# The second product of one batch in matmuls of 256 columns instead of 512, two to a bank

## The chip, the cores and the metric

One core of one Trainium2 chip. The metric is the time of one execution on the device, in microseconds (us); given is the median of a few executions. The engines are TensorE (PE in the profile; its weight loads have a row of their own, PEld), VectorE (DVE), ScalarE (ACT), GpSimd (POOL) and SyncE (SP, which issues nearly all DMAs here).

## The reference

Eight batches of 576 tokens with 8 heads of 64 go through an attention in two steps over 32 packed queries, and then through a feed-forward layer with the gate h * sigmoid(1.702 h). Everything is float32.

```python
def sm_attn(qq, kk, vv):
    s = scale * np.matmul(qq, kk.transpose(0, 1, 3, 2))
    s = s - np.max(s, axis=-1, keepdims=True)
    a = np.exp(s)
    a = a / (np.sum(a, axis=-1, keepdims=True) + 1e-09)
    return np.matmul(a, vv)
p_packed = sm_attn(p, k, v)
out = sm_attn(q, p_packed, p_packed)
...
h = x @ w_in                              # x: 4608 x 512, w_in: 512 x 2048
g = h * (1.0 / (1.0 + np.exp(-1.702 * h)))
return (g @ w_out).astype(np.float32)     # w_out: 2048 x 512
```

## The kernel before

The kernel works batch by batch (B = 8), but its steps are written out by hand in one long table, `order`, in which steps of neighbouring batches alternate: while the feed-forward part of batch 4 runs, the attention of batch 5 and 6 is prepared between its products. Each entry of the table is a function with its arguments, such as `(out_mm, 4, 0, 2)`, and each engine carries out its instructions in the order in which the table issues them.

Precision comes from splitting: a float32 operand is held as a rounded upper part and a lower part, both in the format F32R, and a product is the sum of three: upper x upper, upper x lower, lower x upper.

The attention's last step and the first product of the feed-forward layer are joined: per batch and 512 columns of `w_in` a small matrix m is made (`m_chunk`, PE line L437, tile `psm`), and `h_mm` (L605) multiplies it by the attention's weights. There are 16 column blocks f of 128 and two halves of 288 tokens. Each `h_mm` is six matmuls of 288 columns, with weights of 128x128, into one PSUM bank (tile h, two buffers).

ScalarE then takes the tanh of h (`h_tanh`, L613), VectorE forms the gate (`h_gate`, L595), and two more steps write the upper and lower part of g (`h_upper`, lines L117 and L119; `h_lower`, L592), tiles `ghi` and `glo`, each 128 rows of f by 512 tokens, three buffers. The 64 tokens of a batch beyond 512 are set aside (`h_over`) and worked on in pairs of batches (`over_mm`, tile `acc_over`).

The second product is `out_mm(b, f, i)`: for batch b, block f and token block i (0 to 3, 128 tokens each) it calls `product` (L660 to L667), which issues three matmuls: weights `ghi`, `ghi` and `glo` (128x128 columns of that token block), moving operand the upper, lower and upper part of `w_out`'s block f, all 512 output columns at once. All 16 f of a token block add up in one PSUM bank, `acc0` to `acc3`; the first matmul at f = 0 has start set, the last at f = 15 has stop set. `out_take` then copies the bank to SBUF and `store` writes it out. So a batch has 16 x 4 x 3 = 192 such matmuls. `columns(part)` gives 0:256 for 0, 256:512 for 1 and 0:512 for None; it was there for loading weights by halves.

Of the kernel before, what the change touches and what calls it, by code (L numbers as in the profile page):

```python
# [21 lines left out]
def kernel(  # L22
# [31 lines left out]
    nc = tc.nc  # L54

    P = 128
# [8 lines left out]
    NF = DF // P  # L65
    FC = 512
# [5 lines left out]
    KLAST = S - (KC - 1) * P  # L72
    DEC = 3
    MB = 2
    LATE = [(B - 1, 2)]
    SCALE = 1.0 / float(D) ** 0.5

# [90 lines left out]
    wo = {}  # L168
# [5 lines left out]
    def columns(part):  # L174
        return slice(0, FC) if part is None else slice(part * FC // 2, (part + 1) * FC // 2)
# [276 lines left out]
    def m_upper(b, fc, eo, part=None, engine=nc.scalar):  # L452
        if not part and (b, fc) in LATE:
            if ("late", b, fc) not in st:
                st["late", b, fc] = wk.tile(
                    [P, 2, 2, FC], F32R, tag="late", name=f"late_{b}_{fc}"
                )
            st["m", b, fc, eo] = [st["late", b, fc][:, eo, i, :] for i in range(2)]
        elif not part:
            st["m", b, fc, eo] = [  # L460
                wk.tile([P, FC], F32R, tag=f"{tag}{eo}", name=f"{tag}_{b}_{fc}_{eo}", bufs=MB)
                for tag in ("mhi", "mlo")
            ]
        at = columns(part)
        move(engine, st["m", b, fc, eo][0][:, at], st["bank", "m", b, fc, eo, part][:, at])
# [111 lines left out]
    gs = {}  # L577
    accs = {}
# [81 lines left out]
        src = over_g[pair, i].rearrange("p f t -> p (f t)")  # L660
        lower(g_tiles(("over", pair, i)), 0, src, engine)

    def product(acc, g, f, at, start, stop):
        for i, (part, gp) in enumerate(((0, g[0]), (1, g[0]), (0, g[1]))):
            nc.tensor.matmul(  # L665
                acc, gp[:, at : at + P], wo[f][:, part, :],
                start=(start and i == 0), stop=(stop and i == 2),  # L667
            )

    def acc_bank(i, name):  # L670
        return ps_acc.tile([P, FC], F32, tag=f"acc{i}", name=f"acc{i}_{name}")
# [3 lines left out]
    def out_mm(b, f, i):  # L675
        if f == 0:
            accs[i] = acc_bank(i, f"{b}")
        product(accs[i], gs[b, f], f, i * P, f == 0, f == NF - 1)

    def out_take(b, i, engine=nc.scalar):  # L680
        taken[b, i] = o = o_tile(f"o_{b}_{i}")
# [5 lines left out]
    def over_mm(pair, i):  # L687
        g = gs["over", pair, i]
        if i == 0:
            accs[0] = acc_bank(0, f"over_{pair}")  # L690
        for n in range(CF):
            f = CF * i + n
            product(accs[0], g, f, n * P, f == 0, f == NF - 1)
# [5 lines left out]
    def over_store(pair, k, engine=nc.sync):  # L699
# [38 lines left out]
        (h_upper, 0, 0, 0), (h_lower, 0, 0, 0), (m_chunk, 0, 0, (bank_b, bank_b), 1),  # L738
        (m_upper, 0, 0, 0, 1, dve), (load_w, 5), (bias1, 1, 0), (begin_w, 5), (join_w, 5),
        (h_mm, 0, 0, 1), (m_lower, 0, 0, 0, 1), (out_mm, 0, 0, 0), (h_mm, 0, 1, 1),  # L740
        (h_upper, 0, 1, 0), (h_lower, 0, 1, 0), (load_w, 8), (h_tanh, 0, 0, 1), (out_mm, 0, 0, 1),
        (h_over, 0, 0), (h_gate, 0, 0, 1), (m_upper, 0, 0, 1, 1), (m_lower, 0, 0, 1, 1),
        (h_mm, 0, 2, 0), (upper_w, 5), (h_tanh, 0, 1, 1), (h_gate, 0, 1, 1), (h_over, 0, 1),
        (h_upper, 0, 0, 1), (h_lower, 0, 0, 1, dve), (out_mm, 0, 0, 2), (out_mm, 0, 0, 3),
        (load_w, 6), (begin_w, 6), (join_w, 6), (h_tanh, 0, 2, 0), (lower_w, 5),
        (h_upper, 0, 1, 1), (load_w, 7), (begin_w, 7), (h_gate, 0, 2, 0), (join_w, 7),
# [698 lines left out]
```

## Time and profile before

| | |
|---|---|
| median of 3 runs | 698.31 us (698.3 to 698.85) |
| span of the profiled execution, first to last instruction | 695.4 us (no other time of that execution is given) |
| mean granted TensorE clock | 0.999 |
| matmuls, weight loads | 5022, 5022 |
| of them in the second product | 1536 (8 x 192), and 192 in `acc_over` |
| second product of batch 4 in the trace | about 366 to 444 us |

How to read the rows that follow: a group's row gives line, engine, operation, tiles (out<-in), shapes and count, then busy time, the mean duration of one in ns, and the engine's idle time before them. The chain of waits follows the work that ended last back to the start; here its pieces are listed in order of time as start, length, what, and a count. Matmuls are pipelined: one starts long before the record of the one before it has ended, so a record's duration is not what a matmul costs in a row. F32 matmuls (not F32R) have two records each.

### The profile page before, as it was taken

Reading aid. Unit: us, or ns where it says so; the run is one execution under the profiler, and the core shown is the slowest. Engines: PE = TensorE matmul, PEld = TensorE weight load, DVE = VectorE, ACT = ScalarE, POOL = GpSimd, SP = SyncE. Lnnn points to the kernel's source line nnn. Section 1 sums busy time; section 2 is a strip of 40 time slices with the busy share of each in tenths; the row PEclk is TensorE's granted clock in tenths of the full one; section 3 lists DMA queues with packets and bytes.
Section 4 is the critical chain, followed back from the end, with each engine's and each line's share of the span. In section 5 each row is a group of like instructions: output and inputs, shape, how many; then the busy total and the mean of one; then the engine's idle time right before and its main releaser. Section 6 shows DMA issues by size and latency. Waiting matters only on the chain.

```text
span 695.4 us, 12968 instructions
## 1 busy us (share of the span) xinstructions
PE 685.3 (99%) x5022; PEld 561.1 (81%) x5022; DVE 439.1 (63%) x1111; ACT 258.1 (37%) x620; POOL 96.1 (14%) x115
## 2 busy tenths in 40 slices
PE   7999999999999999999999999999999999999997
PEld 5688788888888888887888878888888887878885
DVE  4988784536555467555686477766785647855443
ACT  3876554423314324433323233332232333333220
POOL 2554372112300224011000000000000000000000
PEclk9999999999999999999999999999999999999999
DMA  8989703432101511064000623034200160010001
GB/s 336 375 307 240 283 1 107 93 113 77 65 1 30 184 65 54 16 155 160 1 31 6 156 56 131 16 110 111 96 16 1 37 177 1 23 40 1 1 15 61
DMA packets 55260, 65.18 MB, mean 94 GB/s; under 512 B 35808, under 2 KB 40864, under 8 KB 54176
## 3 DMA queue, kind: packets, MB, share of 16 engines
q1 hardware_dynamic: 55120, 64.23, 29.2%
q8 instruction: 40, 0.66, 0.4%
q14 instruction: 20, 0.16, 0.1%
q10 hardware_dynamic: 80, 0.13, 0.0%
HBM read 50.78 MB, written 13.57 MB: 93 GB/s over the span
## 4 chain that ended last, share of the span: by engine, by line
PE 93%; DMA 3%; DVE 1%; issue 1%; SPq 1%; ACT 0%; DVEq 0%; ACTq 0%
PE acc L665 50%; PE h L605 28%; PE acc_over L665 5%; PE psm_None L437 4%; DMA aT<-aside 2%; PE pspv L408 1%; PE ps L250 1%; PE ps L495 1%; DMA k<-pk 1%; PE warm L125 1%; SPq L384 1%; DMA aside<-xb 0%; DVE ghi L119 0%; DVE x L506 0%; PE pst L345 0%
## 5 line engine op out<-in xcount | busy, mean ns | idle before, releaser
L665 PE MATMUL acc<-wo,ghi 128*128 128x512 f32 x1024 | 322.9, 397 | 0.0
L665 PEld LDWEIGHTS acc<-wo,ghi 128*128 128x128 f32 x1024 | 179.8, 188 | 40.2 <-issue 11.2
L613 ACT ACTIVATE g<-h 128x288 f32<-128x288 f32 x256 | 104.1, 410 | 278.1 <-PE h L605 262.1
L665 PE MATMUL acc<-wo,glo 128*128 128x512 f32 x512 | 202.0, 395 | 0.0
L595 DVE SCALAR_TENSOR_TENSOR g<-g,h 128x288 f32<-128x288 f32 (+1 forms) x256 | 104.9, 415 | 116.4 <-ACT g L613 115.8
L605 PE MATMUL h<-ahi,mhi 128*128 128x288 f32 x496 | 140.1, 298 | 0.3 <-DVE g L595 0.3
L605 PE MATMUL h<-ahi,mlo 128*128 128x288 f32 x496 | 138.9, 296 | 0.0
L665 PEld LDWEIGHTS acc<-wo,glo 128*128 128x128 f32 x512 | 96.2, 188 | 22.8 <-POOL glo L592 0.4
L605 PEld LDWEIGHTS h<-ahi,mhi 128*128 128x128 f32 x496 | 93.4, 188 | 16.2 <-DVE x L506 4.9
L605 PE MATMUL h<-alo,mhi 128*128 128x288 f32 x496 | 105.2, 293 | 0.0
L605 PEld LDWEIGHTS h<-ahi,mlo 128*128 128x128 f32 x496 | 93.5, 189 | 6.9
L592 DVE TENSOR_TENSOR glo<-g,ghi 128x224 fp32r<-128x224 f32 (+1 forms) x183 | 76.1, 427 | 14.8 <-ACT ghi L117 10.8
L592 POOL TENSOR_TENSOR glo<-g,ghi 128x224 fp32r<-128x224 f32 (+1 forms) x73 | 55.5, 767 | 191.3 <-DVE ghi L119 88.1
L605 PEld LDWEIGHTS h<-alo,mhi 128*128 128x128 f32 x496 | 79.7, 188 | 0.1
L117 ACT CAST ghi<-g 128x288 fp32r<-128x288 f32 (+1 forms) x142 | 55.2, 403 | 54.4 <-DVE g L595 47.6
L595 DVE SCALAR_TENSOR_TENSOR over<-g,h 128x64 f32<-128x64 f32 x128 | 27.0, 214 | 30.6 <-ACT g L613 30.1
L471 DVE TENSOR_TENSOR mlo<-psm_None,mhi 128x512 fp32r<-128x512 f32 x60 | 40.6, 684 | 5.2 <-ACT mhi L117 4.9
L119 DVE CAST ghi<-g 128x224 fp32r<-128x224 f32 (+1 forms) x114 | 35.9, 320 | 7.0 <-PE acc L665 1.4
L665 PE MATMUL acc_over<-wo,ghi_over 128*128 128x512 f32 x128 | 39.9, 393 | 0.0
L117 ACT CAST mhi<-psm_None 128x512 fp32r<-128x512 f32 x45 | 26.2, 584 | 29.3 <-PE psm_None L437 29.3
L437 PE MATMUL psm_None<-w_in,PT 64*32 64x512 f32 x496 | 33.4, 597 | 0.0
L665 PEld LDWEIGHTS acc_over<-wo,ghi_over 128*128 128x128 f32 x128 | 23.6, 188 | 4.8
(95 smaller groups left out, 475.9 us busy)
## 6 DMA issues: line engine op xcount, KB each, us to landing
q<-q SPq DMA_DIRECT2D x16, 576.0 KB, 5.8
v<-v SPq DMA_DIRECT2D x8, 1024.0 KB, 6.2
o<-o SPq DMA_DIRECT2D x32, 256.0 KB, 2.6
raw<-w_out SPq DMA_DIRECT2D x16, 511.8 KB, 6.5
raw<-w_in SPq DMA_DIRECT2D x12, 511.8 KB, 8.9
k<-pk SPq DMA_DIRECT2D x8, 640.0 KB, 4.3
k<-pk SPq DMA_DIRECT2D x8, 576.0 KB, 6.9
aside<-xb SPq DMA_DIRECT2D x56, 72.0 KB, 2.3
```

Of the source, the lines that this page charges most:

```text
L117: nc.scalar.copy(dst, src)
L119: engine.tensor_copy(dst, src)
L125: nc.tensor.matmul(t[:, :P], ident, ident, start=True, stop=True)
L250: nc.tensor.matmul(bank[32 * j : 32 * j + 32, :NH], kq["p", b][rows(eo), j, :], kq["k", b][rows(eo), half, j, :], start=True, stop=True,)
L384: nc.sync.dma_start(d[:, :, NP * eo + j, :], src.rearrange("t (g n) -> t g n", n=NPK))
L437: nc.tensor.matmul(banks[eo][32 * j : 32 * j + 32, columns(part)], PT[rows(eo), j, :], w_in_sb[fc][rows(eo), j, columns(part)], start=True ...
L471: nc.vector.tensor_tensor(lo, bank[:, at], hi.bitcast(F32), op=ALU.subtract)
L592: engine.tensor_tensor(lo, src, hi.bitcast(F32), op=ALU.subtract)
L595: nc.vector.scalar_tensor_tensor(dst, th, 1.0, h, op0=ALU.add, op1=ALU.mult)
L605: nc.tensor.matmul(h[:, :NH], m[eo][part][:, fo : fo + P], a[:, eo * NH : (eo + 1) * NH], start=(n == 0), stop=(n == len(terms) - 1),)
L613: nc.scalar.activation(g, st["h", b, f, half][:, :NH], AF.Tanh, scale=1.702)
L665: nc.tensor.matmul(acc, gp[:, at : at + P], wo[f][:, part, :], start=(start and i == 0), stop=(stop and i == 2),)
```

## The change

For batch 4 alone (`NARROW = 4`) each matmul of the second product becomes two of 256 columns that write the left and the right half of the same bank. The loop over the halves is inside the loop over the three terms, so the order of a product is upper-upper left, upper-upper right, upper-lower left, and so on. The two halves have the same weights, and each has its own weight load. The start flag is on the first half of the first term alone, the stop flag on the last half of the last.

```diff
+    NARROW = 4
...
-    def product(acc, g, f, at, start, stop):
+    def product(acc, g, f, at, start, stop, pieces=(slice(0, FC),)):
         for i, (part, gp) in enumerate(((0, g[0]), (1, g[0]), (0, g[1]))):
-            nc.tensor.matmul(
-                acc, gp[:, at : at + P], wo[f][:, part, :],
-                start=(start and i == 0), stop=(stop and i == 2),
-            )
+            for k, cs in enumerate(pieces):
+                nc.tensor.matmul(
+                    acc[:, cs], gp[:, at : at + P], wo[f][:, part, cs],
+                    start=(start and i == 0 and k == 0), stop=(stop and i == 2 and k == len(pieces) - 1),
+                )
...
-        product(accs[i], gs[b, f], f, i * P, f == 0, f == NF - 1)
+        pieces = (columns(0), columns(1)) if b == NARROW else (slice(0, FC),)
+        product(accs[i], gs[b, f], f, i * P, f == 0, f == NF - 1, pieces)
```

What this does to the order on PE, at two places. First, PE at the first product of batch 4 (f = 0, i = 2), which stands between two `h_mm`; `acc2_4` is bank 2 of batch 4, and in brackets stands what a matmul waits for. Before:

```order
L605 MATMUL h_4_0_2_4347<-alo_4_0_4286,mhi_4_0_1_4148 128x288
L665 MATMUL acc2_4_4358<-wo0_388,ghi_4_0_4319 128x512 [waits Activation_49]
L665 MATMUL acc2_4_4358<-wo0_388,ghi_4_0_4319 128x512
L665 MATMUL acc2_4_4358<-wo0_388,glo_4_0_4320 128x512 [waits DVE_49]
L605 MATMUL h_4_1_2_4365<-ahi_4_1_4186,mhi_4_0_0_3986 128x288 [waits DVE_49]
```

and with the change:

```order
L606 MATMUL h_4_0_2_4347<-alo_4_0_4286,mhi_4_0_1_4148 128x288
L667 MATMUL acc2_4_4358<-wo0_388,ghi_4_0_4319 128x256 [waits Activation_49]
L667 MATMUL acc2_4_4358<-wo0_388,ghi_4_0_4319 128x256 x3
L667 MATMUL acc2_4_4358<-wo0_388,glo_4_0_4320 128x256 [waits DVE_49]
L667 MATMUL acc2_4_4358<-wo0_388,glo_4_0_4320 128x256
L606 MATMUL h_4_1_2_4368<-ahi_4_1_4186,mhi_4_0_0_3986 128x288 [waits DVE_49]
```

Three matmuls became six at the same place, and the waits stay with the first that needs the tile. The second place is PE at the first products of batch 5 in banks 0, 1 and 3, whose columns are not halved. Before:

```order
L665 MATMUL acc0_5_5269<-wo0_388,ghi_5_0_5220 128x512 x2
L665 MATMUL acc0_5_5269<-wo0_388,glo_5_0_5221 128x512
L665 MATMUL acc0_5_5269<-wo1_498,ghi_5_1_5246 128x512 [waits DVE_49]
L665 MATMUL acc0_5_5269<-wo1_498,ghi_5_1_5246 128x512
L665 MATMUL acc0_5_5269<-wo1_498,glo_5_1_5247 128x512 [waits DVE_49]
L665 MATMUL acc1_5_5286<-wo0_388,ghi_5_0_5220 128x512 x2
L665 MATMUL acc1_5_5286<-wo0_388,glo_5_0_5221 128x512
L665 MATMUL acc3_5_5294<-wo0_388,ghi_5_0_5220 128x512 [waits Activation_49]
```

and with the change:

```order
L667 MATMUL acc0_5_5461<-wo0_388,ghi_5_0_5403 128x512 [waits PE_49]
L667 MATMUL acc0_5_5461<-wo0_388,ghi_5_0_5403 128x512
L667 MATMUL acc0_5_5461<-wo0_388,glo_5_0_5404 128x512
L667 MATMUL acc0_5_5461<-wo1_498,ghi_5_1_5438 128x512 [waits DVE_49]
L667 MATMUL acc0_5_5461<-wo1_498,ghi_5_1_5438 128x512
L667 MATMUL acc0_5_5461<-wo1_498,glo_5_1_5439 128x512 [waits DVE_49]
L667 MATMUL acc1_5_5478<-wo0_388,ghi_5_0_5403 128x512 [waits PE_49]
L667 MATMUL acc1_5_5478<-wo0_388,ghi_5_0_5403 128x512
L667 MATMUL acc1_5_5478<-wo0_388,glo_5_0_5404 128x512
L667 MATMUL acc3_5_5486<-wo0_388,ghi_5_0_5403 128x512 [waits PE_49,Activation_49]
```

The work and its order are the same (only the numbers of the tiles differ); three matmuls now also wait for a piece of PE's own earlier work. The orders of DVE, ACT, POOL and SP do not change.

## The prediction

> **What bounds the kernel now.** I read the page first: the busy shares and the granted clock.
>
> ```profile
> span 695.4 us, 12968 instructions
> PE 685.3 (99%) x5022; PEld 561.1 (81%) x5022; DVE 439.1 (63%) x1111; ACT 258.1 (37%) x620; POOL 96.1 (14%) x115
> PEclk9999999999999999999999999999999999999999
> ...
> PE 93%; DMA 3%; DVE 1%; issue 1%; SPq 1%; ACT 0%; DVEq 0%; ACTq 0%
> ```
>
> TensorE (PE) is busy for 99% of the span at a clock that is never throttled, it holds 93% of the chain that ended last (the last row), and every matmul has a weight load of its own (5022 of each). A busy matmul row is not yet a matmul row at its peak, so the next view was the table of stretches, for the stretch that holds the second product of batch 4 (366 to 444 us), together with the groups of that stretch, which show that it holds exactly the 192 matmuls that the change touches.
>
> ```profile
> 366.00:444.00 78.00, 78.00 (x594) 63.80 (x593) 50.27 (x132) 27.39 (x69) 0.00 (x0) 1.00 0.28 78
> L665 PE MATMUL acc<-wo,ghi 128*128 128x512 f32 x128 | 40.3, 396 | 0.0
> L665 PE MATMUL acc<-wo,glo 128*128 128x512 f32 x64 | 25.3, 395 | 0.0
> ACT g L613 <- PE h L605: 38.1, 23, 4.9
> ```
>
> The columns of the first row are stretch, its length, then busy time and count of PE, PEld, DVE, ACT and POOL. PE is busy for all 78.00 us; it waits for nobody there. The last row, from the waits of that stretch, shows the other direction: ScalarE stands idle for 38.1 us until PE delivers h. So nothing in this stretch hides PE time: each nanosecond that PE needs more or less moves the end by as much.
>
> The 395 ns of a matmul in the groups is a latency, start to modelled end; matmuls overlap. What the path pays is the distance from one to the next, and that is read from the chain of waits in order of time (start, us, what). The long unbroken runs of batch 4's stretch:
>
> ```profile
> 371.82 2.79 PE acc L665 x12
> 377.90 4.79 PE acc L665 x21
> 388.83 2.80 PE acc L665 x12
> 392.43 2.08 PE acc L665 x9
> 396.12 3.41 PE acc L665 x15
> 417.76 4.82 PE acc L665 x21
> 430.80 4.89 PE acc L665 x21
> 442.04 2.09 PE acc L665 x9
> ...
> 385.65 1.61 PE h L605 x12
> 394.51 1.61 PE h L605 x12
> 410.14 1.60 PE h L605 x12
> 416.20 1.56 PE h L605 x12
> 422.58 1.56 PE h L605 x12
> 429.21 1.59 PE h L605 x12
> 438.17 1.58 PE h L605 x12
> 440.45 1.58 PE h L605 x12
> ```
>
> The eight runs of 512-column matmuls (acc) hold 120 in 27.67 us: 230.6 ns each. The eight runs of 288-column matmuls (h, the first product, same engine, same kinds of operands, also 128 rows by 128 columns of weights) hold 96 in 12.69 us: 132.2 ns each.
>
> **The change part by part.** It removes 192 matmuls of 512 columns (16 f x 4 token blocks x 3 terms) with their 192 weight loads, and adds 384 of 256 columns with 384 loads. Each pair of halves has the same weights, and they are loaded for each half again.
>
> *The matmuls.* No 128-row matmul of 256 columns in this number format stands in the trace, so its price is drawn through the two widths that do. From 288 to 512 columns the distance grows by 230.6 - 132.2 = 98.4 ns over 224 columns, 0.439 ns a column; going 32 columns below 288 takes off 14.1 ns and gives 118.1 ns. Two of those are 236.2 ns, against 230.6 for the one that they replace: 5.6 ns more. The same line says what that is: at no columns it still stands at 5.7 ns, a fixed price of a matmul that is now paid once more. 192 x 5.6 ns = 1.07 us. All of it is on the path, since PE is never idle in the stretch.
>
> The uncertainty of this term comes from the spread between runs. The steepest line takes the slowest acc run (4.89 us for 21: 232.9 ns) and the fastest h run (1.56 us for 12: 130.0): 0.459 ns a column, 115.3 ns for 256, a pair at 230.6 and so 2.3 ns less than one: -0.44 us. The flattest takes the fastest acc run (3.41 us for 15: 227.3) and the slowest h run (1.61 for 12: 134.2): 0.416 a column, 120.9 for 256, 14.5 ns more a pair: +2.8 us. I take the pooled value, because mixing the fastest of one kind with the slowest of the other is a worst case, and keep both ends for the range.
>
> The Trainium skill, page "TensorE: Matmul & The Clock Gate", section "Back-to-back issue gap", puts the warm distance at N/2.4 + 2.5 ns, hence a fixed price of 2.5 ns. By that rule the sum would be 192 x 2.5 = 0.48 us (an estimate from that page). It gives 215.8 ns for 512 columns where the rows here show 230.6, so I go by the rows.
>
> *The weight loads.* A load lasts 188 ns in its record, longer than the new distance, so I looked for the nearest that loads can follow each other. Before the steady part, warm-up matmuls of 128 columns run back to back:
>
> ```profile
> 16.16 1.41 PEld L125 LDWEIGHTS warm<-ident 128*128 128x128 f32 x12 [0.47 <-issue]
> L665 PEld LDWEIGHTS acc<-wo,ghi 128*128 128x128 f32 x1024 | 179.8, 188 | 40.2 <-issue 11.2
> ```
>
> Twelve loads of 128x128 f32 cover 1.41 us; less the 0.19 us of the last one's record, eleven distances make 1.22 us, 111 ns each. Loads are therefore pipelined, and one every 118 ns can be had, with 7 ns in hand. The matmul hides the next load as now: 0 us. If that cover were gone (loads of the operands here slower than these), the price is the first rival's.
>
> *Instructions and waits.* In the order of the instructions only PE differs. The waits that the 512-column matmuls carried sit on the first half of each term, so no half waits longer than its whole did. Three first matmuls of batch 5 newly name an earlier piece of PE's own work, and one matmul of batch 5 no longer does; that work lies before them in the same queue. Price between 0 and 3 x 0.11 us (a load that cannot be pulled ahead, from the 111 ns above) = 0.33 us; I take 0, since waits of this kind stand before some 45 matmuls already, and PE is busy for 99% of the span with them. Program code is fetched by DMA: 384 instructions at the 63 bytes that the page's rows give,
>
> ```profile
> q8 instruction: 40, 0.66, 0.4%
> q14 instruction: 20, 0.16, 0.1%
> ```
>
> 0.82 MB for 12968, are 24 KB more beside queues that are busy for 0.5%: 0 us. ACT, DVE and the stores of batch 4 get their data up to 1 us later; ACT has 38.1 us of waiting in hand there, and the next work of PE doesn't ask for a store.
>
> *The sum.* 695.4 us of span + 1.07 = 696.5 us. The median of the runs shown, 698.31, lies 2.9 us over that span; nothing of that part is touched. 698.31 + 1.07 = 699.4 us. That is 0.15%, and 0.2% (1.4 us) is about what a measurement of this kernel can tell from no change: the forecast is "within".
>
> **The rivals.** *The weight loads become the bound, and it is slower.* The mechanism: the 132.2 ns of an h matmul might be not its columns but a load that can't be had sooner; then a 256-column matmul also costs 132.2 ns, a pair 264.4, 33.8 ns more than one, 192 x 33.8 = 6.5 us: 704.8 us. It decides as soon as loads of these tiles can't follow within 118 ns, and costs half as much (701.6 us) if they need 124. For it speaks that the record of a load, 188 ns, is longer than the distance; against it the 111 ns of the warm-up loads, of the same 128x128 four-byte shape. Chance 0.10. The Trainium skill, page "Perfetto Trace Analysis", section "Identifying the Most-Contended Engine", has TensorE's headroom judged by the busy share of the weight loads; by that rule a stretch that goes from 63.80 of 78 us towards all of it would have no headroom left, which bears on this rival.
>
> *It is faster.* The excess of a long matmul might not be a straight line: if the fixed price is hidden by shorter matmuls and a half runs at the 111 ns of the closest rows, a pair takes 222, 8.6 ns less than one: -1.65 us, 696.7 us. For it speaks that runs of the same width differ by 2.5% already (227.3 to 232.9), so something beside the columns is in the distance; against it that h, with shorter matmuls, has more time per column, not less (132.2/288 = 0.459 against 230.6/512 = 0.450). Chance 0.05.
>
> *The instruction sequencer becomes the bound.* The stretch issues 594 + 593 = 1187 matmuls and loads in 78.0 us, 65.7 ns each, and would issue 1571. If that were what one takes, down to the 65.0 ns of the fastest h run (24 in 1.56 us), they need 102 to 103 us, 24 to 25 us more: 722 to 723 us. Against it, a run of 80 matmuls with their loads in 1.25 us,
>
> ```profile
> 400.31 1.25 PE pspv L408 x80
> ```
>
> 160 instructions at 8 ns each, though a queue may have held part of them ready. Chance 0.03. The Trainium skill has a sentence that speaks for it, on the page "TensorE: Matmul & The Clock Gate", section "Wait — 56ns, not 53.3ns?": with hardware decode off the sequencer spends about 62 ns on each matmul; were a load to cost the same, that is 97 us for the stretch (an estimate from that page). No row here says which mode this is.
>
> *Half-width matmuls lose the full rate.* The f32 warm-up matmuls take 111 ns for 128 columns, 0.87 ns a column against h's 0.46. If 256 columns of this format fell to that rate, a half would take 222 ns, a pair 444, 192 x 213 ns = 41 us: 739 us. Nothing below 288 columns shows it either way. Chance 0.02.
>
> **How the numbers follow.** The forecast, the fixed price paid twice, has 0.80. Its own bounds are 698.31 - 0.44 = 697.9 and 698.31 + 2.8 = 701.1. I let the range reach to 701.6, half the first rival's price, and leave out the rest of it (about 0.05), the faster case (0.05), the two far ones (0.05) and a tail of 0.05: 697.9 to 701.6. Slower by over 0.2% means above 699.7, an extra of 7.3 ns a pair and so 119.0 ns a half: only 0.9 ns above my value. I give that 0.30 of the forecast's 0.80 (0.24), and nearly all of the three slower rivals (0.15): 0.39. Faster by over 0.2% needs less than 696.9: most of the faster rival, 0.04. Within: 0.57.
>
> **What would show it.** In the profile after, the stretch of batch 4 still has PE busy throughout, about 1.1 us longer; the chain's acc runs there hold 18 or 24 where 9 or 12 stood and give 116 to 121 ns a matmul; h stays at 132. Loads at 118 ns apart with matmuls starting on them say the first rival is gone. Distances of 130 or more in the halves, with the load as what PE waits for, say that I was wrong by it; 111 or less says the faster case; equal distances of load and matmul that hold in the h runs of that stretch too would be the sequencer. If batch 5's first products show PE idle, the three new waits were not free.

## The result, and the profile after

| | before | after |
|---|---|---|
| median of 17 runs | 698.31 us (696.82 to 699.39) | 699.78 us (698.9 to 703.05) |
| ratio, 95% interval | | 1.0025 (1.0016 to 1.0034) |
| span of the profiled execution | 695.4 us | 697.2 us |

The change costs 1.47 us by the medians, and between 1.1 and 2.4 us by the interval. The forecast was 1.07 us more, 0.15%; the measured 0.25% lies on the slower side of the 0.2% that were to be told from no change, but its interval, 0.16% to 0.34%, reaches to both sides of them.

The page after, span and busy times:

```profile
span 697.2 us, 13353 instructions
...
PE 686.7 (98%) x5214; PEld 571.1 (82%) x5214; DVE 439.2 (63%) x1111; ACT 258.4 (37%) x620; POOL 95.7 (14%) x115
```

There are 192 matmuls and 192 loads more, as the order said, and the other engines do what they did. The table of stretches, for the stretch of batch 4 (stretch, length, busy time and count of PE, PEld, DVE, ACT, POOL, then the granted clock, DMA share and GB/s):

```profile
366.00:446.00 80.00, 80.00 (x788) 75.06 (x787) 50.37 (x132) 27.41 (x69) 0.00 (x0) 1.00 0.27 76
```

PE is still never idle there. What grew is its own work, and the weight loads went from 63.80 of 78 us to 75.06 of 80. The chain of waits in order of time shows where (start, us, what); first and last piece of batch 4's second product and the runs that answer to those shown of before:

```profile
367.16 0.71 PE acc L667 x6
...
372.38 2.85 PE acc L667 x24
...
378.54 5.03 PE acc L667 x42
...
389.74 2.88 PE acc L667 x24
...
393.41 2.15 PE acc L667 x18
...
397.15 3.60 PE acc L667 x30
...
419.25 5.04 PE acc L667 x42
...
429.61 1.41 PE acc L667 x12
431.02 1.60 PE h L606 x12
432.63 4.98 PE acc L667 x42
...
440.10 1.58 PE h L606 x12
...
443.99 2.13 PE acc L667 x18
```

The eight runs that correspond hold 240 halves in 28.66 us: 119.4 ns each, where the prediction had 118.1. A pair takes 238.8 ns, 8.2 more than the 230.6 of one matmul before. The h runs stay at 132 ns (1.58 for 12). From the start of the first piece to the end of the last, 367.16 to 446.12, are 78.96 us. Before, the stretch ran from the start of the row below to the end of the run at 442.04 (shown in the prediction), 366.67 to 444.13:

```profile
366.67 0.69 PE acc L665 x3
```

77.46 us, so the stretch grew by 1.50 us, about as much as the medians differ by. Added up over the chain of the stretch, all acc pieces take 46.46 us where they took 45.01, 1.45 more for the 192 pairs; the 186 h matmuls take 25.07 and 25.06, and the other pieces are the same to 0.01 us. The two spans differ by 1.8 us, because batch 4 also begins 0.5 us later, before any changed instruction has run, and what follows the stretch is about 0.1 us shorter. The groups of the loads in that stretch show one more thing, the mean ns of a record, after and before:

```profile
L667 PEld LDWEIGHTS acc<-wo,ghi 128*128 128x128 f32 x252 | 34.7, 190 | 1.4 <-DVE x L120 0.8 <-issue 0.5
L667 PEld LDWEIGHTS acc<-wo,glo 128*128 128x128 f32 x125 | 19.4, 191 | 0.0
```

```profile
L665 PEld LDWEIGHTS acc<-wo,ghi 128*128 128x128 f32 x128 | 22.5, 188 | 4.8 <-DVE x L119 0.8 <-issue 0.5 <-ACT ghi L117 0.2
```

A load lasts 2 to 3 ns longer where the matmul beside it has 256 columns. It is small, but it asks a question that the prediction passed over: is the price one of the matmul, as the word "fixed price of a matmul" had it, or one of the load that each matmul brings with it? In a straight line through two widths the two look the same.

### The profile page after: what moved, and what is told of

Read it like the earlier page. It is cut to its first block, busy times and chain, and to the rows that moved or that the text cites. A ratio compares the mean times of both kernels' runs of the same rounds, so it can differ in the third digit from the quotient of the medians.

```text
span 697.2 us, 13353 instructions
## 1 busy us (share of the span) xinstructions
PE 686.7 (98%) x5214; PEld 571.1 (82%) x5214; DVE 439.2 (63%) x1111; ACT 258.4 (37%) x620; POOL 95.7 (14%) x115
## 4 chain that ended last, share of the span: by engine, by line
PE 95%; DMA 2%; issue 1%; DVE 1%; ACT 0%; SPq 0%; DVEq 0%
PE acc L667 51%; PE h L606 29%; PE acc_over L667 5%; PE psm_None L438 4%; PE ps L251 1%; DMA raw<-w_in 1%; PE pspv L409 1%; PE ps L496 1%; DMA k<-pk 1%; PE warm L126 0%; PE psm L438 0%; DVE mlo L472 0%; SPq L158 0%; ACT mhi L118 0%; DVE g L596 0%
## 5 line engine op out<-in xcount | busy, mean ns | idle before, releaser
L667 PE MATMUL acc<-wo,ghi 128*128 128x512 f32 (+1 forms) x1152 | 323.7, 371 | 0.0
L667 PEld LDWEIGHTS acc<-wo,ghi 128*128 128x128 f32 x1152 | 192.4, 188 | 36.9 <-issue 11.2
L667 PE MATMUL acc<-wo,glo 128*128 128x512 f32 (+1 forms) x576 | 202.4, 369 | 0.0
L667 PEld LDWEIGHTS acc<-wo,glo 128*128 128x128 f32 x576 | 103.9, 188 | 19.9 <-POOL glo L593 0.2
```

The lines of the kernel that those rows point to most:

```text
L667: nc.tensor.matmul(acc[:, cs], gp[:, at : at + P], wo[f][:, part, cs], start=(start and i == 0 and k == 0), stop=(stop and i == 2 and k == ...
```

## The experiments

Theory A is the prediction's: a matmul costs a fixed 5.7 ns and 0.439 ns a column, whatever its weights. Theory B: the load has a pace of its own, and the price is paid where the load lasts nearly as long as the matmul that hides it. They part where matmuls are narrower still, and where loads are shorter.

**All eight batches in halves.** The batch is no longer asked for:

```diff
-        pieces = (columns(0), columns(1)) if b == NARROW else (slice(0, FC),)
+        pieces = (columns(0), columns(1))
```

> All eight batches have their second product in halves of 256 columns. Price per matmul that is split (both theories): the trace after gives 119.4 ns a half where one of 512 took 230.6, so 8.2 ns more, 8 x 192 x 8.2 = 12.6 us, 710.9 us, ratio 1.018. If the time of the one batch came from its place in the order or from the three new waits, not from the split, the ratio stays well under that; by the straight line of the prediction (118.1 ns) it is 8 x 1.07 = 8.6 us, 706.9 us, ratio 1.012.

Measured: 708.99 us against 698.62 us of the kernel before on the same chip, ratio 1.0141 (1.0121 to 1.0162): 8.5 to 11.3 us, 1.1 to 1.4 us a batch. So the price goes with the number of matmuls that are split, and the place in the order or the waits of batch 5 are not its cause. The 12.6 us expected from the long unbroken runs of the chain are too many, as the interval ends at 11.3; the 1.45 us of all acc pieces, times eight, are 11.6, and the 8.6 us of the prediction's line lie just inside the interval. The profile alone would have said 13.0 (a span of 708.4 us against 695.4), but it is of the slowest of the four executions, 710.27 us.

**Other widths.** Each batch has its own list of widths:

```diff
+    WIDTHS = {1: (128, 128, 128, 128), 2: (288, 224), 3: (320, 192), 4: (256, 256), 5: (352, 160), 6: (384, 128)}
...
+        at, pieces = 0, []
+        for n in WIDTHS.get(b, (FC,)):
+            pieces.append(slice(at, at + n))
+            at += n
```

> The second product in other widths: batch 1 in 4 x 128 columns, batch 2 in 288 + 224, batch 3 in 320 + 192, batch 4 in 2 x 256, batch 5 in 352 + 160, batch 6 in 384 + 128, the rest whole. Theory A, a fixed price per matmul and a straight line below it (5.7 ns + 0.439 ns a column): 128 columns take 62 ns, 160 76, 192 90, 224 104; batch 1 gets 17.1 ns a term longer and the others 5.7, together 192 x (17.1 + 5 x 5.7) = 8.8 us, about 707 us. Theory B, the next weight load is a floor of about 120 ns however narrow the matmul is: each of the narrow pieces takes 120 ns, batch 1 grows by 192 x (480 - 230.6) = 47.9 us, batches 2 to 6 by 4.1, 6.8, 1.6, 9.6 and 12.2 us, together 82 us, about 780 us. Theory C, narrow F32R matmuls fall below the full rate: pieces under 256 take more than 120 ns (222 for 256 at the rate of the f32 warm-up), more than 780 us.

Measured: 766.8 us in one run, 68 us over the 698.62 of before; A's 707 is far off and B's 780 too high. The chain of this run: batch 1 (4 x 128), then batch 2 (288 + 224), batch 3 (320 + 192), batch 5 (352 + 160) and batch 6 (384 + 128), some of the longest runs of each:

```profile
182.29 7.99 PE acc L667 x72
...
210.41 13.35 PE acc L667 x120
...
308.88 5.13 PE acc L667 x42
...
340.71 4.64 PE acc L667 x36
...
524.13 4.83 PE acc L667 x36
...
660.05 5.12 PE acc L667 x36
```

Matmuls of 128 columns follow each other every 111 ns (13.35 us for 120), not every 62: there is a floor, at 111 to 112 ns rather than the 120 of the expectation, and it is the distance that the prediction read from the warm-up loads. The uneven pairs fit the same floor. A pair of 288 + 224 takes 244.3 ns (5.13 us for 21 pairs), 320 + 192 take 257.8 (4.64 for 18), 352 + 160 take 268.3 (4.83 for 18), 384 + 128 take 284.4 (5.12 for 18). The floor for the narrow piece and the line for the wide one, 112 + 132.2, 112 + 146.2, 112 + 160.2 and 112 + 174.3, give 244, 258, 272 and 286, the last two 4 and 2 more than measured. The sum of what each batch then costs over 230.6 ns a term, 192 x (213.4 + 13.7 + 27.2 + 8.2 + 37.7 + 53.8) ns with 4 x 111 and 238.8 for batches 1 and 4, is 68 us, as much as was measured. A narrow piece saves nothing by being narrow, and what the wide piece beside it has to spare does not make up for it. Whether the 111 to 112 ns belong to the load or to the matmul as such, this run does not say. Theory A has fallen for pieces below 256 columns. Theory C (a lower rate for narrow matmuls) falls by the uneven pairs: at the 0.87 ns a column of the f32 warm-up, 224 columns would take 194 ns and a pair of 288 + 224 326, not 244.3. The 111 ns of 128 columns alone would not have refuted it, as that rate gives 111 there too.

**Shorter loads.** `product` gets the number of weight columns, and batch 6 has the loops turned round:

```diff
+    PLAN = {1: (64, (256, 256)), 2: (64, (512,)), 3: (64, (128, 128, 128, 128)), 4: (128, (256, 256)), 5: (128, (176, 168, 168))}
+    APART = 6
...
-                    acc[:, cs], gp[:, at : at + P], wo[f][:, part, cs],
+                    acc[:, cs], gp[:, at : at + n], wo[f][:, part, cs],
...
+        if b == APART:
+            for cs in (columns(0), columns(1)):
+                for k, (part, gp) in enumerate(((0, gs[b, f][0]), (1, gs[b, f][0]), (0, gs[b, f][1]))):
...
+        n = P if f in (0, NF - 1) else n
+        product(accs[i][:n], gs[b, f], f, i * P, f == 0, f == NF - 1, pieces, n)
```

> In batches 1, 2 and 3 the weights have 64 columns instead of 128 for f = 1 to 14, which leaves out half of the tokens of these batches there; the moving operand is 2 x 256, 1 x 512 and 4 x 128 columns. Batch 4 as in the change, batch 5 in 176 + 168 + 168 columns, batch 6 in halves with the loop over the halves outside the three terms. Theory A (fixed price per matmul): 64-column weights change nothing, 256 stay at 119 to 120 ns, 512 at 231; 128 take 62. Theory B (load floor): the load of 64 columns takes half as long, about 60 ns, so 256 columns fall to the straight line, 118 ns, or a little below, 128 columns to about 62 to 65; and batch 5's pieces, with full loads, take 120 ns each, 360 a term (by A 242). If the floor is one of a matmul's issue and not of the load's columns, 128 columns with 64-column weights also take about 120 ns. Batch 6: as batch 4 in both; if adding twice in a row into the same 256 columns of a bank costs something, it is longer than batch 4.

Measured: 728.91 us in one run. The chain of this run: batch 1 (64 columns of weights, 2 x 256), batch 2 (64, 512), batch 3 (64, 4 x 128), batch 5 (128, 176 + 168 + 168) and batch 6 (halves outside):

```profile
135.45 3.42 PE acc L668 x30
...
157.38 4.10 PE acc L668 x36
...
264.99 4.82 PE acc L668 x21
...
316.46 2.88 PE acc L668 x48
...
334.02 3.60 PE acc L668 x60
...
486.94 6.00 PE acc L668 x54
...
624.55 4.27 PE acc L689 x36
...
633.32 4.29 PE acc L689 x36
```

With loads of 64 columns, 256 columns take 114.0 ns (3.42 us for 30), not 119.4, and 128 columns take 60.0 (3.60 for 60), not 111: the floor is the load's, and with 64 columns it lies at 60 ns or lower. Whole matmuls of 512 columns gain next to nothing by the short load, 229.5 ns (4.82 for 21) against 230.6. At 114 ns for 256 the fixed price is gone: two of them, 228 ns, are no longer than one of 512. One thing is not separated: with 64 columns of weights a matmul also writes only 64 rows of the bank (`accs[i][:n]`). That 512 columns hardly gain by it, and that with full loads pieces of 128, 168 and 176 columns all take 111 ns, however much they write, speaks for the load. Thirds of 176 and 168 columns with full loads take 111.1 ns each (6.00 for 54), on the floor, where theory B had 120. Turning the loops round changes nothing: 118.6 to 119.2 ns, and the same batch with the usual loops in the next experiment has the same 4.27 us for 36. So adding three times in a row into the same 256 columns of a bank cost nothing here. The 60.0 ns also settle the prediction's rival of the sequencer: 60 matmuls and 60 loads in 3.60 us are 30 ns an instruction, half of the 65.7 by which it would have bound this stretch.

**How long the load may be.** The same code with six lengths of weights under halves of 256:

```diff
+    PLAN = {1: (32, (256, 256)), 2: (64, (256, 256)), 3: (96, (256, 256)), 4: (112, (256, 256)), 5: (120, (256, 256)), 6: (128, (256, 256))}
```

> Second product in halves of 256 columns with weights of 32, 64, 96, 112, 120 and 128 columns in batches 1 to 6 (f = 1 to 14; the tokens beyond these columns are left out there). Theory B, refined: a load of 128 columns needs 112 ns (128-column matmuls follow at 111.7 in the widths), and 256 columns alone need 114.6 (with 64-column weights); what makes 120 of them is the load running nearly as long. Then 32, 64 and 96 columns give 114 to 115, and the distance rises only at 112 to 128 columns, to 120. Theory A (a fixed price of a matmul) is already weakened: it would have 119 to 120 everywhere. A third, that every column of weights read slows the matmul beside it: the distance rises evenly, about 0.08 ns a column: 112, 115, 117, 118, 119, 120.

Measured: 701.07 us in one run. The groups of the loads by shape show their records' mean ns in the column after the comma:

```profile
L667 PEld LDWEIGHTS acc<-wo,ghi 128*120 128x120 f32 x224 | 30.1, 181 | 1.0 <-issue 0.9
L667 PEld LDWEIGHTS acc<-wo,ghi 128*112 128x112 f32 x224 | 29.6, 174 | 0.6 <-issue 0.5
L667 PEld LDWEIGHTS acc<-wo,ghi 128*96 128x96 f32 x224 | 28.8, 161 | 1.3 <-ACT x L118 0.8 <-issue 0.5
L667 PEld LDWEIGHTS acc<-wo,ghi 128*64 128x64 f32 x224 | 26.9, 134 | 1.4 <-issue 1.4
L667 PEld LDWEIGHTS acc<-wo,ghi 128*32 128x32 f32 x224 | 24.0, 108 | 2.9 <-issue 1.3
```

From 32 to 120 columns the record grows by 73 ns over 88 columns, 0.83 ns a column. If only the part of the record that grows with the columns keeps the next load waiting, a load of 128 columns needs 0.83 x 128 = 106 ns of its 188 (an estimate from these rows), which fits the floor of 111. One run of the chain for each of 32, 96, 120 and 128 columns:

```profile
134.95 3.42 PE acc L667 x30
...
329.12 3.49 PE acc L667 x30
...
494.08 2.81 PE acc L667 x24
...
596.72 4.27 PE acc L667 x36
```

They give 114.0, 116.3, 117.1 and 118.6 ns. All runs of 24 and more, pooled, give 115.4 ns at 32 columns, 115.5 at 64, 116.4 at 96, 116.6 at 112, 118.5 at 120 and 119.3 at 128. (They hold some matmuls of f = 0 and 15 with full loads.) Each length has a batch of its own, but the batch is not what makes the difference: with full loads everywhere, in the first experiment, runs pooled in the same way give 119.3 to 120.8 ns in batches 1 to 6. The distance is flat to 64 columns and then rises by some 4 ns; the steps between 64 and 112 are not sure, as the long runs at 112 columns alone lie between 113.6 and 118.0. The refined theory B expected it flat to 96, the third theory an even rise from 112; neither curve is quite it, and how a load that is not yet the longer of the two lengthens the distance stays open. That the length of the load decides holds in both.

**The short loads, timed in several runs.** All eight batches with 64 columns of weights, once whole and once in halves:

```diff
+    PLAN = {b: (64, (512,)) for b in range(8)}
```

```diff
+    PLAN = {b: (64, (256, 256)) for b in range(8)}
```

> All eight batches with weights of 64 columns at f = 1 to 14 and whole matmuls of 512 columns (half of the tokens is left out there). PE's order and count are those of before. By both theories about the time of before: 512 columns took 230.1 with short loads against 231.1, so 1344 x 1.0 = 1.3 us less, 697.2 us, ratio 0.998.

> As the run with short loads and whole matmuls, but in halves of 256 columns in all eight batches. Theory A, the price is one of a matmul: 10.4 us over the whole ones as with full loads, 707.5 us. Theory B, the price is the load's: at f = 1 to 14 a pair takes 2 x 114.6 = 229.2 against 230.1, 1344 x -0.9 = -1.2 us; at f = 0 and 15, with full loads, 192 x 8 = +1.5 us; together 0.3 us over the whole ones, 697.5 us, ratio to before 0.999.

Measured: whole 698.4 us, ratio to before 0.9999 (0.9989 to 1.0009); in halves 695.82 us, ratio 0.9961 (0.9946 to 0.9976). With short loads the split that costs 10.4 us with full ones costs nothing; the halves are 2.6 us faster. Theory A's 707.5 us is out. One run of batch 4's chain each, in halves and then whole:

```profile
416.07 4.78 PE acc L667 x42
```

```profile
420.34 4.85 PE acc L667 x21
```

113.8 ns a half, 227.6 a pair, against 231.0 whole. Halves were expected 0.3 us over the whole ones, since f = 0 and 15 still pay for full loads; they are 2.6 us under them. All long unbroken runs of that batch pooled (29.64 us for 258 halves, 29.84 for 129 whole ones) give 229.8 ns against 231.3, which would be 2.3 us over 1536 terms. These two profiles don't explain it, though: the h matmuls, alike in both kernels, take 17.48 us for 132 in that of the halves (runs of 12 in this stretch) and 17.71 in that of the whole ones, a larger difference in proportion, and the first is of the fastest execution of its kernel, the second of the slowest. The 2.6 us rest on the medians, and why they are more than the expectation had is open.

## Why the prediction was right, and where not

- **PE bounds the stretch and nothing hides it**: held. PE is busy for all of the stretch after too, and the 1.50 us by which the stretch grew agree with the 1.47 us of the medians, with h and the other work unchanged.
- **The distance of 256 columns, 118.1 ns by the line through 288 and 512**: mis-sized by 1.3 ns. The chain has 119.4, so a pair costs 8.2 ns more, not 5.6, and 192 of them 1.57 us, not 1.07 (all acc pieces together: 1.45). That lay inside the bounds given (115.3 to 120.9) and left the time inside the range, but it moved the distance over the 119.0 ns, and the median 0.1 us over the 699.7 us, at which the prediction ended "within"; the interval leaves open on which side of that line the change lies.
- **What the line said it was, a fixed price of a matmul**: wrong. With 64-column loads the price is gone (114.0 ns at 256 columns, and 695.82 against 698.4 us for eight batches). It comes with the load of 128 columns, which can be had every 111 ns, nearly the whole time of a 256-column matmul. With short loads 256 and 512 columns both cost 0.45 ns a column (114.0 and 229.5 ns). At that rate 288 columns would take about 129 ns (an estimate) where h, with full loads, takes 132.2; so the line's lower point probably held some of the price and its upper one none, which made the line flatter and left 5.7 ns at no columns. No run shortened h's loads to show it.
- **Luck in the size**: the line happened to pass 1.3 ns from the measured distance at 256 columns. The same line puts 128 columns at 62 ns, where 111 were measured, so it would have failed a little further down.
- **The loads have 7 ns in hand, cost 0**: half right. The 111 ns read from the warm-up loads are the floor, found again at 128 columns (111 ns), and 256 columns stay above it. But a load that fits is not free: with full loads a 256-column matmul takes 119.4 ns, with loads of half the columns 114.0.
- **Rivals**: the first (loads as the bound, 132.2 ns) did not happen at 256 columns, although the records of the loads then cover 75.06 of 80 us; its mechanism is real below that, with the floor at 111, and costs 41 us for one batch at 4 x 128 (192 x (4 x 111 - 230.6) ns). The faster case (111 ns a half) didn't come: a half takes 119.4 ns, and even with short loads about 114. The sequencer is out by 30 ns an instruction, the loss of the full rate by 119.4 ns.
- **Three new waits in batch 5, at 0**: held. The chain has the first twelve matmuls of batch 5's second product, with all three places among them, in 2.77 us after and before; first after, then before:

```profile
447.70 2.77 PE acc L667 x12
```

```profile
445.69 2.77 PE acc L665 x12
```

## What to carry to other kernels

Where every matmul brings its own weights, as here, its price was the longer of two paces, columns of the moving operand and columns of the load, and a few ns more where they come close. Read the pace of the loads from the closest that any loads in the trace follow each other, before cutting matmuls narrower. A line through two widths finds the size of such a price, but only a run with a shorter load tells whose price it is.

## What the runs showed of the hardware

A load of 128 columns (F32R, 128 rows) can be had every 111 ns, one of 64 columns every 60 ns or less; the record of a load grows by 0.83 ns a column from 108 ns at 32. Below that pace a narrower matmul saves nothing: 384 + 128 columns take 284 ns where 256 + 256 take 239 and 512 take 231, although all three have the same columns to stream.
